# Full contraction depth for every matmul, and a part of the output scaling moved to ScalarE

## The chip, the core and the metric

The kernel runs on one core of a Trainium2 chip. The metric is the device time of one execution in microseconds. The kernel before takes 212.89 us, the median of three runs (211.91 to 213.91); one execution that was recorded by the profiler spans 211.2 us from the first to the last instruction.

## The reference

The input `A_u` is a sequence of 2048 positions with 512 channels. Two layers work on it, and a gate mixes them:

```python
x = A_u                                            # (1, 2048, 512), bf16
g = sigmoid((x * gate_w).sum(-1, keepdims=True))
a = conv(x)                                        # long convolution, below
b = x + scatter(two routed tokens)                 # below
return g * a + (1 - g) * b

# conv: a kernel of 2048 taps per channel, from 128 complex modes
K = einsum("dn,dnl,dn->dl", C, exp(dt * A * l), dt * B).real
y = irfft(rfft(pad(x)) * rfft(pad(K)))[:L] + x * Dskip

# routing: the two positions with the largest x @ w_r pass a gated MLP
y = (silu(x_sel @ w_gate) * (x_sel @ w_up)) @ w_down * sigmoid(r_sel)
b = x + scatter_add(y at the two positions)
```

The kernel does the Fourier transforms as matmuls with constant cosine and sine tables, in two blocks of 1024 positions and two halves of 256 channels. The taps are the product of two small tables of exponentials: one over coarse lags, one over fine lags.

## The kernel before

The kernel has a small scheduler of its own. Each step is recorded with the buffers that it reads and writes and with a cost; a list scheduler then decides the order on each engine, and for some steps also the engine (`EV`, an eviction from PSUM, and `SCL`, a scaling, may go to ScalarE or to VectorE). [...] So a change of a cost or of a step can change the order of the whole program. The helpers `TT`, `STT`, `CP` are VectorE operations, `AC` is a ScalarE activation; because a helper records the operation, the profile gives them all the helper's line (387 for `TT`, 394 for `STT`, 398 for `AC`, 402 for `EV`, 406 for `SCL`).

The order of the parts in the program, cut to what the steps below touch:

```python
exps1(0); exps2(0)       # all exponentials, ScalarE
# ... a part of them is parked in HBM ("park") and read back for the second half
routing()                # transposes of x, gate, the top two, the MLP
tab1(0, (1, 1))          # sine and cosine times exponentials: coarse table, half 0
forward()                # Fourier transform of x
tab2(0, (1, 1))          # fine table, half 0
tab1(1, (1, 1))
xupd()                   # x + routed rows, scaled by 1 - g
kgen(0)                  # product of the tables, then selection
# ... DMA of the spectrum matrix KP and of the parked table
tab2(1, (1, 1))
kspec(0)                 # spectrum of the taps, half 0
kgen(1)
products(0, 0); products(0, 1)   # spectrum products, VectorE
# ... DMA of the inverse matrix G
kspec(1)
inverse(0)               # inverse transform, gate and add
products(1, 0); products(1, 1)
inverse(1)
```

In the product of the tables and the selection, a group of lags is brought together onto 32 partitions; the identity matrix, every fourth column of it, is the stationary operand. The first of the four groups also takes `Dskip` in, by a matmul of one row:

```python
def kgen(h):
    # ... 64 x 2 matmuls of 84 columns in 11 groups, each evicted to KA[h]
    for bk in range(3):
        pb = misc()
        def sel(hh, bk=bk, pb=pb):
            njg = 2 if bk < 2 else 1
            for g in range(4):
                for c4 in range(4):
                    lw = CB(0, 128, c4, (4, 32))
                    last = hh.matmul(pb(32 * g, 32, c4, (256, njg), (4, 64)), lw, KA[h](...),
                                     start=True, stop=(bk + g > 0), tile_position=(0, 32 * g))      # line 767
                    if bk + g == 0:
                        last = hh.matmul(pb(0, 32, c4, (4, 64)), CB(0, 1, 0, (1, 32)), DSK(0, 1, h * HC + c4, (4, 64)),
                                         start=False, stop=True, tile_position=(0, 0))              # line 770
            if bk == 2:
                for c4 in range(4):
                    last = hh.matmul(pb(0, 32, 256 + c4, (4, 64)), CB(0, 128, c4, (4, 32)), KA[h](...),
                                     start=True, stop=True, tile_position=(0, 0))                   # line 773
        # ... bk 0 and 1 evicted whole; bk 2 in two pieces, of 128 and of 32 partitions
```

The spectrum of the taps uses blocks of 128 rows, and for the last block (the single lag 2048 steps on) 32 rows. `KUSE` has five uses for `i == 0`, all of 128 rows, and two for `i == 1`, of 128 and of 32 rows:

```python
KUSE = [(0, 0), (0, 1), (0, 2), (0, 3), (0, 4), (1, 4), (1, 5)]
def kspec(h):
    for qd in range(2):
        for i in range(2):
            # ... for each of two parts, four rows of the spectrum:
            for n, tau in enumerate(taus):
                for k, u in enumerate(uses):
                    jg = KUSE[u][1]
                    np_ = 128 if jg < 5 else 32
                    last = hh.matmul(pb(0, 128, n * 256, (1, 256)), KP(0, np_, ...), KC[h](0, np_, jg * 256, (1, 256)), ...)  # line 795
```

The update with the routed rows alternates a matmul of 128 rows and one of two rows, and ScalarE scales the sum:

```python
def xupd():
    for tb in range(16):
        # pb: one of two PSUM buffers, c0: one of its halves
        h.matmul(pb(0, 128, c0, (1, D)), IDN(0, (1, 128)), U(0, 128, tb * D, (1, D)), start=True, stop=False)          # line 871
        h.matmul(pb(0, 128, c0, (1, D)), OHR(0, 2, tb * 128, (1, 128)), ZB(0, 2, D, (1, D)), start=False, stop=True)   # line 872
        AC(U(...), pb(...), ACTF.Copy, ..., scale=SG(0, 128, 48 + tb, (1, 1)))
```

The inverse transform is 16 matmuls for each group of two tiles of positions (line 845). For the first half of the channels ScalarE scales with the gate into `YA`, and VectorE adds four tiles at once. For the second half VectorE does both in one operation per tile:

```python
if h == 0:
    for e in range(2):
        AC(YA(...), pb(...), ACTF.Copy, ..., scale=SG(0, 128, 32 + tb, (1, 1)))
    if t2 == 1:
        u = U(0, 128, (blk * 8 + par) * D, (2 * D, 4), (1, HC))
        TT(u, u, YA(0, 128, par * 1024, (HC, 4), (1, HC)), ADD, ...)
    continue
for e in range(2):
    STT(u, pb(0, 128, e * 256, (1, 256)), SG(0, 128, 32 + tb, (1, 1)), u, MUL, ADD, ...)
```

Of the kernel before, what the change touches and what calls it, by code (L numbers as in the profile page):

```python
# [326 lines left out]
def bass_gated_mix__ssm_conv_s4__moe_arch_mod__prompt_kernel(nc, A_u, A_A_re, A_A_im, A_B_re, A_B_im, A_C_re, A_C_im, A_log_dt, A_Dskip,  # L327
# [4 lines left out]
    sgn = np.diag(np.where(np.arange(128) % 2 == 0, 1.0, -1.0))  # L332
    cb = np.concatenate([eye, sgn, -sgn], 1)
    cb_c = const(cb, "c_bf")
# [17 lines left out]
    with ExitStack() as es:  # L352
# [59 lines left out]
        def small(name, nbytes, dt):  # L412
            b = B(name, o_[0], nbytes, dt)
            o_[0] += (nbytes + 31) // 32 * 32
            return b
        CB = small("cb", 768, BF); CF = small("cf", 640, F32); AL = small("al", 2048, F32); B16 = small("b16", 2048, F32)
        WW = small("ww", 2048, BF); SG = small("sg", 256, F32); SGB = small("sgb", 128, BF); RTS = small("rts", 1088, F32)
# [66 lines left out]
        DQ([(LDT(0, 128, 0, (1, D)), dr(A_log_dt, 0, (0, 128), (1, D)))], [], [LDT], 131072, eng=ACT)  # L484
        DQ([(CB(0, 128, 0, (1, 384)), cb_c[:, :])], [], [CB], 98304, eng=ACT)
        P.op(ACT, ld_w, [], [WL], cost=1.0, n=2, nbytes=20000, dma=True, prio=2.5e5)
# [8 lines left out]
        for ft in range(2):  # L495
            DQ([(NG[ft](0, 128, 0, (128, 8), (1, 128)), ngsrc(ft))], [], [NG[ft]], 262144)
        DQ([(WG(0, 128, 0, (NF, 4), (1, NF)), dr(B_w_gate, 0, (NF, 128), (128 * NF, 4), (1, NF)))], [], [WG], 1835008)
        DQ([(DSK(0, 1, 0, (1, D)), dr(A_Dskip, 0, (D, 1), (1, D)))], [], [DSK], 1024)

# [116 lines left out]
        def routing():  # L616
            for q in range(8):
                bb = misc(True)
                def tr(h, q=q, bb=bb):
                    last = None  # L620
                    for t_ in range(2):
                        for db in range(4):
                            last = h.transpose(bb(0, 128, db * 256 + t_ * 128, (1, 128)), U(0, 128, (2 * q + t_) * D + db * 128, (1, 128)), IDN(0, (1, 128)))  # L623
                    return last
                P.op(PE, tr, [(U, 2 * q), (U, 2 * q + 1), CB], [bb.buf], cost=0.7)
                EV(XT(0, 128, q * 256, (L, 4), (1, 256)), bb(0, 128, 0, (256, 4), (1, 256)), [bb.buf], [(XT, q)])
            b = misc()
            def lg(h):
# [7 lines left out]
                return last  # L636
            P.op(PE, lg, [XT, WL], [b.buf], cost=64 * 0.03)
            CP(SGB(0, 128, 0, (1, 16)), b(0, 128, 0, (2, 16)), [b.buf], [(SGB, "s")])
# [33 lines left out]
            def gat(h):  # L672
# [4 lines left out]
                return last  # L677
            P.op(PE, gat, [U, OHT], [gb.buf], cost=64 * 0.03)
            CP(XS(0, 128, 0, (1, 8)), gb(0, 128, 0, (1, 8)), [gb.buf], [XS])
            for hf in range(2):  # L680
                bb = misc(True)
                def tro(h, bb=bb, hf=hf):
                    last = None
                    for t_ in range(8):
                        last = h.transpose(bb(0, 2, t_ * 128, (1, 128)), OHT(0, 128, (hf * 8 + t_) * 2, (1, 2)), IDN(0, (1, 128)))
                    return last
                P.op(PE, tro, [OHT, CB], [bb.buf], cost=0.7)
                EV(OHR(0, 2, hf * 1024, (1, 1024)), bb(0, 2, 0, (1, 1024)), [bb.buf], [(OHR, hf)])
# [3 lines left out]
            for i, (W, k) in enumerate(((wg, [WG]), (wu, WU))):  # L692
                bb = misc()
                def ffn1(h, W=W, bb=bb):
                    last = None
                    for fb in range(14):
                        for db in range(4):
                            last = h.matmul(bb(0, 128, fb * 2, (1, 2)), W(db, fb), XS(0, 128, db * 2, (1, 2)), start=(db == 0), stop=(db == 3))
                    return last
                P.op(PE, ffn1, [*k, XS], [bb.buf], cost=56 * 0.035)  # L700
                CP(hb(i), bb(0, 128, 0, (1, 28)), [bb.buf], [(HB, i)])
# [4 lines left out]
            def dn(h):  # L706
# [3 lines left out]
                return last  # L710
            P.op(PE, dn, [(HB, 3), WD], [yb.buf], cost=14 * 0.24)
            CP(ZB(0, 2, 0, (1, D)), yb(0, 2, 0, (1, D)), [yb.buf], [(ZB, 0)])
# [3 lines left out]
        def forward():  # L716
            np_ = [0]
            for blk in range(NBLK):
                for ft in range(4):
# [4 lines left out]
                    for pm in range(2):  # L724
                        pb = fwp[np_[0] % 2]
                        np_[0] += 1
                        for part in range(2):
                            def fw(h, blk=blk, ft=ft, pm=pm, pb=pb, ng=ng, part=part):
# [6 lines left out]
                                if blk:  # L735
                                    last = h.matmul(o, CB(0, 128, 128 * (2 if part == 0 else 1), (1, 128)),
                                                    X(0, 128, (1 - part) * 2048 + (pm * 4 + ft) * 256, (8192, 2), (1, 256)), start=False, stop=True)
                                return last
                            rd = [F, CB, ng] + [(U, blk * 8 + t) for t in range(8)]
                            if blk:  # L740
                                rd += [xk(hh, 0, 1 - part, pm, ft) for hh in range(2)]
                            P.op(PE, fw, rd, [(pb.buf, part)], cost=(8 + blk) * 0.22)
                        EV(X(0, 128, blk * 4096 + (pm * 4 + ft) * 256, (2048, 2), (8192, 2), (1, 256)), pb(0, 128, 0, (512, 2), (256, 2), (1, 256)),
                           [pb.buf], [xk(hh, blk, part, pm, ft) for hh in range(2) for part in range(2)])

        def kgen(h):
            for b0 in range(0, 64, 6):
                ng = min(6, 64 - b0)
                pb = kgp[(b0 // 6) % 2]
                def mm(hh, b0=b0, ng=ng, pb=pb):  # L750
# [5 lines left out]
                    return last  # L756
                P.op(PE, mm, [*TP[h], *TQ[h]], [pb.buf], cost=ng * 2 * 0.05)
                EV(KA[h](0, 128, b0 * 84, (1, ng * 84)), pb(0, 128, 0, (1, ng * 84)), [pb.buf], [(KA[h], b0)])
            for bk in range(3):
                pb = misc()  # L760
                def sel(hh, bk=bk, pb=pb):
                    last = None
# [4 lines that stand above are left out]
                            last = hh.matmul(pb(32 * g, 32, c4, (256, njg), (4, 64)), lw, KA[h](0, 128, c4 + 4 * (8 * bk + g), (16, njg), (84, 64)),  # L767
                                             start=True, stop=(bk + g > 0), tile_position=(0, 32 * g))
                            if bk + g == 0:
                                last = hh.matmul(pb(0, 32, c4, (4, 64)), CB(0, 1, 0, (1, 32)), DSK(0, 1, h * HC + c4, (4, 64)), start=False, stop=True, tile_position=(0, 0))  # L770
                    if bk == 2:
                        for c4 in range(4):
                            last = hh.matmul(pb(0, 32, 256 + c4, (4, 64)), CB(0, 128, c4, (4, 32)), KA[h](0, 128, c4 + 80, (84, 64)),
                                             start=True, stop=True, tile_position=(0, 0))
                    return last
                P.op(PE, sel, [KA[h], CB, DSK], [pb.buf], cost=16 * 0.09)
                if bk < 2:
                    EV(KC[h](0, 128, bk * 512, (1, 512)), pb(0, 128, 0, (1, 512)), [pb.buf], [(KC[h], bk)])
                else:
                    EV(KC[h](0, 128, 1024, (1, 256)), pb(0, 128, 0, (1, 256)), [pb.buf], [(KC[h], 2)])  # L780
                    EV(KC[h](0, 32, 1280, (1, 256)), pb(0, 32, 256, (1, 256)), [pb.buf], [(KC[h], 3)])
        def kspec(h):
            for qd in range(2):
                for i in range(2):
                    uses = [u for u, (bi, jg) in enumerate(KUSE) if bi == i]
                    pb = fwp[i]
                    for part in range(2):
                        taus = [part * 8 + pm * 4 + 2 * qd + e for pm in range(2) for e in range(2)]
                        def ks(hh, taus=taus, uses=uses, pb=pb):
                            last = None  # L790
                            for n, tau in enumerate(taus):
                                for k, u in enumerate(uses):
                                    jg = KUSE[u][1]
                                    np_ = 128 if jg < 5 else 32
                                    last = hh.matmul(pb(0, 128, n * 256, (1, 256)), KP(0, np_, u * 2048 + tau * 128, (1, 128)), KC[h](0, np_, jg * 256, (1, 256)), start=(k == 0), stop=(k == len(uses) - 1))  # L795
                            return last
                        P.op(PE, ks, [KP, KC[h]], [pb.buf], cost=4 * len(uses) * 0.115)
                        o = KK[h](0, 128, i * 4096 + part * 2048 + 2 * qd * 256, (1024, 2), (1, 512))
# [35 lines left out]
        def inverse(h):  # L834
            for blk in (1, 0):
                for par in range(2):
                    for t2 in range(2):
                        pb = ivb[ni[0] % 4]
                        ni[0] += 1
                        def iv(hh, blk=blk, par=par, t2=t2, pb=pb):  # L840
# [6 lines left out]
                            return last  # L847
                        P.op(PE, iv, [G] + [xk(h, blk, part, par, ft) for part in range(2) for ft in range(4)], [pb.buf], cost=16 * 0.115)
                        if h == 0:
                            for e in range(2):  # L850
                                tb = blk * 8 + (2 * t2 + e) * 2 + par
                                AC(YA(0, 128, (2 * t2 + e) * 256 + par * 1024, (1, HC)), pb(0, 128, e * 256, (1, HC)), ACTF.Copy, [pb.buf, (SG, "g")], [(YA, (par, t2, e))], scale=SG(0, 128, 32 + tb, (1, 1)))
                            if t2 == 1:
                                tbs = [blk * 8 + s_ * 2 + par for s_ in range(4)]
                                u = U(0, 128, (blk * 8 + par) * D, (2 * D, 4), (1, HC))
                                TT(u, u, YA(0, 128, par * 1024, (HC, 4), (1, HC)), ADD, [(YA, (par, a_, e)) for a_ in range(2) for e in range(2)] + [(U, ("x", tb)) for tb in tbs], [(U, ("o", tb, h)) for tb in tbs])
# [9 lines left out]
        def xupd():  # L866
            for tb in range(16):
                pb = fwp[(tb // 2) % 2]
                c0 = (tb % 2) * 512
                def xu(h, tb=tb, pb=pb, c0=c0):  # L870
                    h.matmul(pb(0, 128, c0, (1, D)), IDN(0, (1, 128)), U(0, 128, tb * D, (1, D)), start=True, stop=False)  # L871
                    return h.matmul(pb(0, 128, c0, (1, D)), OHR(0, 2, tb * 128, (1, 128)), ZB(0, 2, D, (1, D)), start=False, stop=True)  # L872
                P.op(PE, xu, [(U, tb), CB, OHR, (ZB, 1)], [(pb.buf, tb % 2)], cost=0.5)
# [81 lines left out]
```

## Time and profile before

| | before |
|---|---|
| time, median of 3 | 212.89 us (211.91 to 213.91) |
| span of the profiled execution | 211.2 us |
| TensorE (PE) busy | 180.4 us, 1490 matmuls |
| TensorE weight loads (PEld) busy | 109.8 us |
| VectorE (DVE) busy | 173.8 us |
| ScalarE (ACT) busy | 138.1 us |
| mean granted TensorE clock | 0.911 |
| spectrum matmuls of 32 rows | 32, 278 ns mean |
| selection: 128 rows / 1 row | 96 + 8 of line 773 / 8 |
| update: 128 rows / 2 rows | 16 / 16 |

Three engines are busy for most of the span, in a program of several stages, so the shares say little. A matmul's duration in the records is from its start to the modelled end of its passage through the array; matmuls overlap, and what a stream of them costs is the distance between starts. "Idle before" is the time that an engine stood still ahead of an instruction, with the engine or DMA that ended it behind the arrow. TensorE's granted clock is 1.00 or 0.50 at any moment; a figure between is the mean of a stretch.

By stage: the exponentials on ScalarE fill the first 34 us. From 36 to 99 us VectorE (60.2 of 62.9 us) and ScalarE (58.9) build the tables while TensorE does the forward transform. Then come selection, update and spectrum of the first half, the tables of the second half, products and inverse transforms.

### The profile page before, as it was taken

How to read it: one execution, taken by the hardware profiler on the slowest of the kernel's cores; microseconds unless marked ns; L12 is line 12 of the kernel's file. 1: busy time of each engine (PE TensorE's matmuls, PEld its weight loads, DVE VectorE, ACT ScalarE, POOL GpSimd, SP SyncE). 2: the span in 40 equal slices, each digit the busy share in tenths (PEclk: the TensorE clock that was granted, in tenths of full speed). 3: DMA queues.
4: the chain of work that ended last, by engine and by line, in shares of the span. 5: the costliest groups of instructions: out<-in, count | busy, mean ns of one | idle time of the engine just before them, and what ended most of it. 6: DMA issues, size and time to landing. Idle time of an engine off the chain costs nothing.

```text
span 211.2 us, 3613 instructions
## 1 busy us (share of the span) xinstructions
PE 180.4 (85%) x1490; PEld 109.8 (52%) x1490; DVE 173.8 (82%) x292; ACT 138.1 (65%) x221; POOL 0.2 (0%) x4
## 2 busy tenths in 40 slices
PE   0294999999999999997997999849889999936992
PEld 0273446743444444463341366529556777825882
DVE  0889465999999999975259969999997969998952
ACT  3899999999889996999279745526534455430000
POOL 0000000000000000000000000000000000000000
PEclk9996699979999999999797589975969999996999
DMA  5999996290202201001990000000370000213033
GB/s 96 357 286 350 373 388 205 55 339 7 50 4 49 50 7 42 3 0 25 432 429 14 0 3 0 0 0 3 90 310 0 0 3 0 73 30 99 0 99 99
DMA packets 22097, 23.08 MB, mean 109 GB/s; under 512 B 13121, under 2 KB 19394, under 8 KB 21442
## 3 DMA queue, kind: packets, MB, share of 16 engines
q1 hardware_dynamic: 20738, 22.63, 32.4%
q10 hardware_dynamic: 1344, 0.23, 0.9%
q8 instruction: 11, 0.18, 0.4%
q14 instruction: 4, 0.03, 0.0%
HBM read 18.93 MB, written 3.15 MB: 105 GB/s over the span
## 4 chain that ended last, share of the span: by engine, by line
DVE 40%; PE 32%; ACT 22%; DMA 3%; SPq 1%; issue 1%; DVEq 0%
DVE AR L387 33%; ACT AR L398 15%; PE ps L845 9%; PE ps L795 8%; ACT AR L402 5%; PE ps L767 4%; PE ps L754 3%; DVE AR L391 3%; DMA AR<-in_A_u_dram 3%; PE ps L623 2%; PE ps L734 2%; PE ps L872 1%; PE ps L871 1%; DVE AR L402 1%; DVE AR L406 1%; SPq L483 1%
## 5 line engine op out<-in xcount | busy, mean ns | idle before, releaser
L387 DVE TENSOR_TENSOR AR<-AR 128x1024 bf16<-128x1024 bf16 (+6 forms) x182 | 134.6, 798 | 19.2 <-DMA AR<-in_A_A_re_dram 5.2
L402 ACT ACTIVATE AR<-ps 128x1024 bf16<-128x1024 f32 (+7 forms) x59 | 45.5, 787 | 34.0 <-PE ps L795 19.9
L734 PE MATMUL ps<-AR 128*128 128x512 bf16 x256 | 63.3, 400 | 0.0
L398 ACT ACTIVATE AR<-AR 128x512 bf16<-128x512 f32 (+3 forms) x84 | 59.3, 770 | 5.2 <-DVE AR L391 3.7
L734 PEld LDWEIGHTS ps<-AR 128*128 128x128 bf16 x256 | 25.6, 102 | 31.6 <-issue 5.9
L795 PE MATMUL ps<-AR 128*128 128x256 bf16 x224 | 33.8, 288 | 1.8 <-ACT AR L402 1.8
L845 PE MATMUL ps<-AR 128*128 128x256 bf16 x256 | 30.2, 282 | 4.9 <-DVE AR L387 4.9
L845 PEld LDWEIGHTS ps<-AR 128*128 128x128 bf16 x256 | 25.5, 101 | 9.1 <-DVE AR L387 5.2
L795 PEld LDWEIGHTS ps<-AR 128*128 128x128 bf16 x224 | 22.2, 101 | 13.6 <-ACT AR L402 2.6
L398 ACT ACTIVATE AR<-ps,AR 128x512 bf16<-128x512 f32 (+1 forms) x32 | 17.1, 582 | 7.4 <-PE ps L845 7.0
L406 ACT ACTIVATE AR<-AR 128x256 int32<-128x256 f32 (+1 forms) x44 | 19.1, 492 | 0.2
L754 PE MATMUL ps<-AR 128*128 128x84 bf16 x256 | 13.8, 221 | 4.9 <-DVE AR L387 2.9
L754 PEld LDWEIGHTS ps<-AR 128*128 128x128 bf16 x256 | 12.6, 110 | 7.7 <-ACT AR L402 3.7
L623 PE MATMUL ps<-AR 128*128 128x128 bf16 x64 | 6.4, 278 | 9.9 <-DMA AR<-in_A_u_dram 9.4
L391 DVE TENSOR_SCALAR AR<-AR 128x1024 int32<-128x1024 int32 (+4 forms) x24 | 13.2, 550 | 0.3
L623 PEld LDWEIGHTS ps<-AR 128*128 128x128 bf16 x64 | 5.4, 127 | 10.8 <-DMA AR<-in_A_u_dram 9.4
L394 DVE SCALAR_TENSOR_TENSOR AR<-ps,AR 128x256 bf16<-128x256 f32 x16 | 7.0, 478 | 4.6 <-PE ps L845 4.6
L406 DVE TENSOR_SCALAR AR<-AR 128x256 int32<-128x256 f32 (+1 forms) x28 | 7.0, 292 | 2.8 <-ACT AR L398 2.7
L767 PE MATMUL ps<-AR 128*32 128x128 bf16 (+1 forms) x96 | 8.4, 381 | 0.7 <-ACT AR L402 0.7
L402 DVE CAST AR<-ps 128x1024 bf16<-128x1024 f32 (+1 forms) x6 | 6.7, 1124 | 2.1 <-PE ps L734 2.1
L871 PE MATMUL ps<-AR 128*128 128x512 bf16 x16 | 7.3, 455 | 1.3 <-ACT AR L398 1.3
L872 PE MATMUL ps<-AR 2*128 2x512 bf16 x16 | 7.4, 465 | 0.0
(35 smaller groups left out, 54.4 us busy)
## 6 DMA issues: line engine op xcount, KB each, us to landing
AR<-c_ksp SPq DMA_DIRECT2D x1, 3584.0 KB, 13.8
AR<-in_A_u_dram SPq DMA_DIRECT2D x2, 1024.0 KB, 7.0
AR<-c_fwd SPq DMA_DIRECT2D x1, 2048.0 KB, 8.1
AR<-c_fwdn SPq DMA_DIRECT2D x8, 256.0 KB, 3.9
AR<-c_inv SPq DMA_DIRECT2D x1, 2048.0 KB, 7.8
out_dram<-AR SPq DMA_DIRECT2D x16, 128.0 KB, 2.2
AR<-in_B_w_gate_dram SPq DMA_DIRECT2D x1, 1792.0 KB, 11.0
AR<-in_B_w_up_dram SPq DMA_DIRECT2D x2, 896.0 KB, 11.4
```

What stands on the lines that cost most here:

```text
L387: return P.op(DVE, lambda h: h.tensor_tensor(out=o, in0=a, in1=b, op=op), rd, wr, cost=tt_cost(o, a, b), **k)
L391: return P.op(DVE, lambda h: h.tensor_scalar(out=o, in0=a, scalar1=s1, scalar2=None, op0=op0), rd, wr, cost=c, **k)
L398: return P.op(ACT, lambda h: h.activation(out=o, in_=a, func=func, scale=scale, bias=bias), rd, wr, cost=0.185 + nel(o) * 0.833e-3 + (0.09 ...
L402: return P.op((ACT, DVE), (lambda h: h.activation(out=o, in_=a, func=ACTF.Copy), lambda h: h.tensor_copy(o, a)), rd, wr, cost=(0.185 + n * ...
L406: return P.op((ACT, DVE), (lambda h: h.activation(out=o, in_=a, func=ACTF.Copy, scale=c), lambda h: h.tensor_scalar(out=o, in0=a, scalar1= ...
L623: last = h.transpose(bb(0, 128, db * 256 + t_ * 128, (1, 128)), U(0, 128, (2 * q + t_) * D + db * 128, (1, 128)), IDN(0, (1, 128)))
L734: last = h.matmul(o, w, U(0, 128, (blk * 8 + st * 2 + par) * D, (1, D)), start=(par + st == 0), stop=(par * 4 + st == 7 and blk == 0))
L754: last = hh.matmul(pb(0, 128, (g - b0) * 84, (1, 84)), TP[h][1 - part](0, 128, g * 128, (1, 128)), TQ[h][1 - part](0, 128, g * 84, (1, 84) ...
L767: last = hh.matmul(pb(32 * g, 32, c4, (256, njg), (4, 64)), lw, KA[h](0, 128, c4 + 4 * (8 * bk + g), (16, njg), (84, 64)), start=True, sto ...
L795: last = hh.matmul(pb(0, 128, n * 256, (1, 256)), KP(0, np_, u * 2048 + tau * 128, (1, 128)), KC[h](0, np_, jg * 256, (1, 256)), start=(k ...
L845: last = hh.matmul(pb(0, 128, e * 256, (1, 256)), G(0, 128, ((par * 2 + part) * 4 + ft) * 512 + (2 * t2 + e) * 128, (1, 128)), X(0, 128, h ...
L872: return h.matmul(pb(0, 128, c0, (1, D)), OHR(0, 2, tb * 128, (1, 128)), ZB(0, 2, D, (1, D)), start=False, stop=True)
```

## The change

Every matmul is given 128 rows. The one-row skip operand, the two-row one-hot operands and the 32-row spectrum operands are held in buffers of 128 partitions whose other rows are zero: `DSK`, `OHR` and `ZB` are cleared by GpSimd at the start, and the last selection group is written to all 128 partitions by a stationary operand that has zero columns beyond the 32 (the identity table gets 384 zero columns for it). The sums are the same. [...] Besides, the scaling of one of the two blocks of the second half goes to ScalarE, as in the first half, and a dozen costs for the scheduler are new.

```diff
-    cb = np.concatenate([eye, sgn, -sgn], 1)
+    cb = np.concatenate([eye, np.zeros((128, 384), np.float32), sgn, -sgn], 1)
...
+        for buf, n in ((DSK, D), (OHR, L), (ZB, 2 * D)):
+            P.op(POOL, lambda h, buf=buf, n=n: h.memset(buf(0, 128, 0, (1, n)), 0.0), [], [buf], cost=0.2 + n * 0.5e-3)
...
-                P.op(PE, tr, [(U, 2 * q), (U, 2 * q + 1), CB], [bb.buf], cost=0.7)
+                P.op(PE, tr, [(U, 2 * q), (U, 2 * q + 1), CB], [bb.buf], cost=0.9)
... (costs of the logits, gather, MLP, forward, table, spectrum and inverse matmuls: 1 to 26% lower)
-                P.op(PE, tro, [OHT, CB], [bb.buf], cost=0.7)
+                P.op(PE, tro, [OHT, CB], [bb.buf], cost=0.5)
...
-  last = hh.matmul(pb(0, 32, c4, (4, 64)), CB(0, 1, 0, (1, 32)), DSK(0, 1, h * HC + c4, (4, 64)), start=False, stop=True, tile_position=(0, 0))
+  last = hh.matmul(pb(0, 32, c4, (4, 64)), CB(0, 128, 0, (1, 32)), DSK(0, 128, h * HC + c4, (4, 64)), start=False, stop=True, tile_position=(0, 0))
...
-  last = hh.matmul(pb(0, 32, 256 + c4, (4, 64)), CB(0, 128, c4, (4, 32)), KA[h](0, 128, c4 + 80, (84, 64)), start=True, stop=True, tile_position=(0, 0))
+  last = hh.matmul(pb(0, 128, 256 + c4, (4, 64)), CB(0, 128, c4, (4, 128)), KA[h](0, 128, c4 + 80, (84, 64)), start=True, stop=True)
...
-                if bk < 2:
-                    EV(KC[h](0, 128, bk * 512, (1, 512)), ...)
-                else:
-                    EV(KC[h](0, 128, 1024, (1, 256)), ...)
-                    EV(KC[h](0, 32, 1280, (1, 256)), ...)
+                EV(KC[h](0, 128, bk * 512, (1, 512)), ...)
...
-                                    np_ = 128 if jg < 5 else 32
-  last = hh.matmul(pb(...), KP(0, np_, u * 2048 + tau * 128, (1, 128)), KC[h](0, np_, jg * 256, (1, 256)), ...)
+  last = hh.matmul(pb(...), KP(0, 128, u * 2048 + tau * 128, (1, 128)), KC[h](0, 128, jg * 256, (1, 256)), ...)
...
-                        if h == 0:
+                        if h == 0 or blk == 1:
...
-  return h.matmul(pb(0, 128, c0, (1, D)), OHR(0, 2, tb * 128, (1, 128)), ZB(0, 2, D, (1, D)), start=False, stop=True)
+  return h.matmul(pb(0, 128, c0, (1, D)), OHR(0, 128, tb * 128, (1, 128)), ZB(0, 128, D, (1, D)), start=False, stop=True)
```

Ahead of the change ScalarE evicts two of the eight groups of transposes of x among its exponentials, and after it three; the order of the table matmuls, the update and the last forward blocks differs too.

## The prediction

> **What bounds the kernel now.** I read first the chain that ended last, by engine: VectorE carries 40% of it, although TensorE is busy longer. Then the timeline of VectorE alone, where a bracket gives the idle time before a piece and who ended it. These lines are the whole pieces from 98.9 us on that begin with idle time, up to the last stretch:
>
> ```profile
> 103.90 1.29 DVE L387 TENSOR_TENSOR AR<-AR 128x1024 bf16<-128x1024 bf16 x2 [4.95 <-DMA AR<-park]
> 108.20 3.10 DVE L387 TENSOR_TENSOR AR<-AR 128x1024 bf16<-128x1024 bf16 x5 [3.01 <-PE ps L773]
> ...
> 124.79 1.83 DVE L387 TENSOR_TENSOR AR<-AR 128x2048 bf16<-128x2048 bf16 x2 [1.82 <-ACT AR L402]
> ...
> 162.09 9.43 DVE L387 TENSOR_TENSOR AR<-AR 128x2048 bf16<-128x2048 bf16 x10 [1.56 <-ACT AR L402]
> 173.28 21.19 DVE L387 TENSOR_TENSOR AR<-AR 128x1024 bf16<-128x1024 bf16 x26 [1.76 <-ACT AR L398]
> ```
>
> VectorE works from 36.3 to 194.5 us with hardly another gap. So TensorE matters where it ends one of these gaps, and in the last stretch: from 191.66 us TensorE runs 128 matmuls in 15.76 us and everything waits for them. The third view is the chain in order of time, around the second gap (selection, line 767; its K=1 skip matmul, line 770) and the third (first group of the spectrum, line 795):
>
> ```profile
> 103.25 0.33 PE ps L767
> 103.58 0.15 PE ps L770
> ...
> 105.20 2.54 PE ps L767 x42
> 107.74 0.44 PE ps L773 x4
> ...
> 119.59 4.12 PE ps L795 x20
> 123.71 0.02 issue
> 123.73 1.03 ACT AR L402
> ```
>
> A selection matmul beside a K=1 one costs 0.33 and its partner 0.15 us; 42 of them without partners take 0.06 us each. The same is seen in two stretches of equal clock, counted by windows (the count is that of matmuls): full-depth matmuls of 256 columns, and the alternation of K=128 with K=32:
>
> ```profile
> 161.04:163.02 1.98, 1.98 (x20) 1.00 0.00 0
> 163.02:164.71 1.69, 1.69 (x11) 1.00 0.00 0
> ```
>
> The single starts in the trace are 0.109 us apart in the first stretch and 0.211 to 0.216 us in the second. The routing update (lines 871 and 872, K=128 and K=2) steps by 0.32 us per 512-column matmul at full clock, where the plain forward stream steps by about 0.216 (8 in 1.89 us less the pipeline's tail). In each case an alternation adds about 0.10 us per matmul.
>
> [...] the 0.10 us above is paid exactly where the number of rows changes[...]. [...] Here 2x128 loads take 93 ns and 128x128 ones 99 to 102, so zero rows cost nothing by themselves. [...] The windows' granted clock here is 0.50 or 1.00; TensorE ran 116 to 124 us fully "busy" at 0.50 and 0.59, with the K=2 alternation in it. [...]
>
> **The change, part by part.**
>
> 1. Spectrum. 32 of 224 matmuls go from 32 to 128 rows; each stands beside a 128-row one, 8 of 28 per group. Per group 8 x (0.211-0.109) = 0.8 us, 8 groups: 6.5 us of TensorE time.
> 2. Selection. Four pairs took 4 x 0.48 = 1.93 us. As 8 equal matmuls on one column tile they take 0.06 each (the row of 42) to 0.12 each (L773, four on one tile): 0.5 to 1.0. Saved 0.9 to 1.4, say 1.3 us, twice. The last four, now 128 columns wide, I leave equal; one eviction instead of two (0.60 against 0.64).
> 3. Routing update: 32 matmuls x 0.10 = 3.4 us of TensorE time, but ScalarE's eviction (0.58 net each) sets much of that pace.
> 4. Scaling of one of the two blocks of the second half: 8 VectorE pieces of 0.48 become 8 ScalarE pieces of 0.47 and two adds of 0.6. In the last stretch TensorE steps 0.109 us x 128 whatever VectorE does: worth 0.
> 5. Zero fills on GpSimd: it is otherwise empty, and they come before any reader. Identity table 192 instead of 96 KB: at 345 GB/s about 0.3 us for the first input behind it.
> 6. The scheduler's costs change, so the order changes. Evictions of the transposes on ScalarE go from 2 to 3 before the exponentials end. ScalarE is the chain there, so +0.9 us, and about +0.3 us for waiting for that transpose (the second one now comes early). VectorE now runs two one-hot evictions (0.6 each) ahead of the negated sine at 36.31 us. The table stretch starts about 1.6 us later; VectorE has three 0.2 us scalings fewer, so about +1.0 remains at 83 us.
>
> **From there to the end.** At 83 us ScalarE takes over. Up to the last kernel-table eviction the new order removes from it two cosines and one sine (2.9), five scalings (1.5), one forward eviction (0.9), adds three update evictions (1.8), and makes it wait some 2.3 us for a forward block that is now ahead of the tables. Adding its pieces from 82.4 us gives the last table matmul at 98.3, against 99.03 now.
>
> After it: an update pair, one forward block (1.95 us at full clock, 3.45 at half, as at 99.5 to 103 now), then selection 4.9-1.3 = 3.6, gives 104.4 to 105.9; the parked table's DMA (lands 4.8 us after issue) and one 1.13 us eviction that VectorE gets put its restart at 104.5 in any case. Now it is 108.20. I take 105.2: **-3.0**.
>
> From the selection's end VectorE has 14.8 us of work, plus one 0.6 us multiply that now comes before it: 15.4. The first spectrum eviction was ready 16.6 us after the selection's end. In the new order ScalarE does the last update evictions by 12.3, TensorE needs 2.2 us warm or 4.1 cold for 20 matmuls, and the eviction 1.0: 14 to 16. The 1.82 us gap shrinks to about nothing: 16.6-15.4 = **-1.2**.
>
> For the gap at 162.09 VectorE waits for the second spectrum group. TensorE's path to it loses 1.3 (selection) and 0.8 (first 8 of K=32), 2.1 against a gap of 1.56: **-1.6**. For the gap at 173.28 (scaled output of the first half) TensorE's path loses two more groups of 8, 1.6 us, and has 0.5 left over from the gap before (2.1-1.6): enough for the whole 1.76 if all goes well. I take **-1.5**.
>
> In the last stretch TensorE then stands idle longer than the present 4.9 us, and it begins at half clock, now for 3.3 us (16 matmuls at 0.21 instead of 0.11, 1.6 us lost). [...] **+0.6**.
>
> Sum: -3.0-1.2-1.6-1.5+0.6 = -6.7, from 212.89: **206.2 us**.
>
> **Rivals.** (a) The gaps are filled by other waits. For it: VectorE is at 96% from 36 to 99 us and nothing there is removed, every gap has a second arrival close behind, and the DMA of the parked table caps the first. Then 1 or 2 us remain: 211. Against: all four arrivals come from TensorE's stream in stages that the change shortens.
> (b) The order costs more at the front than the gaps give: ScalarE +1.2, VectorE +1.6 before 40 us, and ScalarE saturated to 99. If none of it is recovered by the table evictions, the second gap gains 1 instead of 3: 208 to 210.
> (c) The clock. The clock falls to half seven times before the end. If full rows count as busier, the update and first spectrum stay at full clock from 108 to 124 us, and TensorE's path there is 4 us shorter. But VectorE's 15.4 us is already the longer path, so little more comes; only a warm selection stage and a warm table stretch would help, 203 to 204. Against a general gain: the half-clock windows at 140 and 191 us follow idle time, which remains.
> (d) The moved scaling is the main thing: it would show as an earlier end of the last stretch. TensorE's unbroken 15.74 us there speaks against it.
>
> **Range and chances.** The gaps add to 8.1 us from 108 on; all gained and the front free is 203.5; half gained with a late front is 209.5. Eight in ten: 203.3 to 209.8. The 2% line is 208.6; I put 0.80 on faster, 0.17 within, 0.03 slower, the last because nothing added is long.
>
> **What would show it.** Spectrum matmuls all 0.109 us apart, and no 1- or 2-row form; selection in about 3.6 us; VectorE's four gaps of 3.0, 1.8, 1.6, 1.8 us at most 0.5 each; last stretch of 15.5 to 17.5 us of TensorE as before. I am wrong if zero-padded matmuls keep the 0.2 us step [...], if VectorE's restart after the selection is later than 107 us, or if new gaps of over 1 us stand in VectorE between 40 and 90 us.

## The result, and the profile after

| | before | after |
|---|---|---|
| time, median of 4 | 212.44 us (211.91 to 213.91) | 205.55 us (205.34 to 207.2) |
| ratio, with 95% interval | | 0.9682 [0.9609, 0.9754] |
| span of the profiled execution | 211.2 us | 203.5 us |
| last stretch (128 matmuls) begins | 191.66 us | 183.08 us |
| mean granted TensorE clock | 0.911 | 0.921 |

The change is worth 6.9 us of the medians. The predicted 206.2 us is 0.65 us too high, and the range holds the result.

VectorE's timeline after the change, columns as before: start, length, what, and in brackets the idle time ahead of the piece and who ended it.

```profile
104.64 4.30 DVE L387 TENSOR_TENSOR AR<-AR 128x1024 bf16<-128x1024 bf16 x7 [0.58 <-PE ps L775]
...
114.88 73.67 DVE L387 TENSOR_TENSOR AR<-AR 128x1024 bf16<-128x1024 bf16 x96
190.18 0.69 DVE L387 TENSOR_TENSOR AR<-AR 128x1024 bf16<-128x1024 bf16 x1 [1.63 <-ACT AR L398]
```

The wait of 3.01 us for the selection is 0.58 us, and VectorE restarts at 104.64 us instead of 108.20. The three gaps after it (1.82, 1.56, 1.76 us) have no successors: one unbroken piece of 73.67 us reaches to 188.5 us, into the last stretch. This accounts for the difference of the two profiled executions. The restart is 3.56 us earlier, the three gaps give 5.14, and the rest of VectorE's time between the restart and the last stretch is 0.12 longer (78.44 us, against 83.46 less 5.14). Together 8.58 us, which is 191.66 less 183.08. The last stretch gives 0.92 back; 7.66 us remain, the difference of the spans.

The chain in order of time, around the first selection (line 769; 772 is the former one-row matmul, 775 the last group), the spectrum (791) and the last stretch (841), columns start, length, what:

```profile
98.92 1.73 PE ps L736 x8
...
100.87 0.33 PE ps L769
101.20 0.06 PE ps L772
101.26 0.24 PE ps L769
101.50 0.06 PE ps L772
101.56 2.45 PE ps L769 x43
104.01 0.61 PE ps L775 x4
...
158.85 3.06 PE ps L791 x28
...
183.08 16.68 PE ps L841 x128
```

The same parts of the chain before (734 is the forward transform, 795 the spectrum, 845 the inverse transform):

```profile
99.60 3.43 PE ps L734 x8
...
166.74 3.78 PE ps L795 x28
...
191.66 15.76 PE ps L845 x128
```

The former one-row matmul takes 0.06 us instead of 0.15, and the matmul behind it 0.24 instead of 0.33. A selection takes 3.75 us instead of 4.9. A group of 28 spectrum matmuls takes 3.06 us, 0.109 each; before it took 3.78. Only the last four of the selection are dearer, 0.61 us against 0.44. The last stretch is 16.68 us, against 15.76.

Not all of the earlier restart belongs to the change. The 3.56 us divide into 0.59 for the earlier end of the table matmuls, 0.09 for an update pair, 1.18 for the selection, and 1.70 for the eight forward matmuls between them, which ran at half clock before (3.43 us) and at full clock after (1.73). The kernel with the moved scaling alone (below), which has the order of the kernel before up to there, ran this block at full clock, and its VectorE waited 1.34 us for the selection instead of 3.01. First its chain, then its VectorE:

```profile
99.80 1.83 PE ps L734 x8
```

```profile
106.80 3.10 DVE L387 TENSOR_TENSOR AR<-AR 128x1024 bf16<-128x1024 bf16 x5 [1.34 <-PE ps L773]
```

Against that execution the restart is 2.16 us earlier, and the spans differ by 5.8 us (209.4 against 203.5).

The chain by engine, from the page:

```profile
PE 63%; DVE 22%; ACT 7%; DMA 4%; issue 1%; SPq 1%; DVEq 0%
```

Before, VectorE had 40% of it. It has not become idle (171.3 us busy, 173.8 before). The share follows the order of the program and not the length of the waits: in the new order with the short rows back, where the waits are back too, TensorE has 69%, and in the old order with full rows VectorE has 55%.

### The profile page after: what moved, and what is told of

It is laid out like the page before. It is cut to its first block, busy times and chain, and to the rows that moved or that the text cites. A ratio compares the mean times of both kernels' runs of the same rounds, so it can differ in the third digit from the quotient of the medians.

```text
span 203.5 us, 3609 instructions
## 1 busy us (share of the span) xinstructions
PE 163.9 (81%) x1479; PEld 108.6 (53%) x1490; DVE 171.3 (84%) x281; ACT 141.1 (69%) x232; POOL 3.4 (2%) x7
## 4 chain that ended last, share of the span: by engine, by line
PE 63%; DVE 22%; ACT 7%; DMA 4%; issue 1%; SPq 1%; DVEq 0%
PE ps L736 28%; DVE AR L387 20%; PE ps L841 12%; PE ps L791 6%; PE ps L756 5%; ACT AR L402 4%; DMA AR<-in_A_u_dram 4%; PE ps L769 3%; ACT AR L398 3%; PE ps L738 2%; PE ps L711 2%; PE ps L625 1%; PE ps L700 1%; SPq L483 1%; PE ps L637 1%
## 5 line engine op out<-in xcount | busy, mean ns | idle before, releaser
L387 DVE TENSOR_TENSOR AR<-AR 128x1024 bf16<-128x1024 bf16 (+7 forms) x184 | 135.7, 797 | 12.5 <-DMA AR<-in_A_A_re_dram 6.8
L398 ACT ACTIVATE AR<-AR 128x512 bf16<-128x512 f32 (+4 forms) x84 | 59.5, 769 | 5.4 <-DVE AR L391 2.1
L402 ACT ACTIVATE AR<-ps 128x1024 bf16<-128x1024 f32 (+4 forms) x56 | 44.0, 811 | 25.5 <-PE ps L791 12.8
L736 PE MATMUL ps<-AR 128*128 128x512 bf16 x248 | 59.0, 388 | 0.8 <-issue 0.5
L841 PE MATMUL ps<-AR 128*128 128x256 bf16 x256 | 31.1, 287 | 5.9 <-DVE AR L387 5.9
L398 ACT ACTIVATE AR<-ps,AR 128x256 bf16<-128x256 f32 (+1 forms) x40 | 20.4, 565 | 18.8 <-PE ps L841 18.8
L841 PEld LDWEIGHTS ps<-AR 128*128 128x128 bf16 x256 | 26.3, 103 | 10.2 <-DVE AR L387 6.2
L791 PE MATMUL ps<-AR 128*128 128x256 bf16 x224 | 26.1, 274 | 1.7 <-ACT AR L402 1.7
L406 ACT ACTIVATE AR<-AR 128x256 int32<-128x256 f32 (+1 forms) x50 | 21.1, 484 | 0.1
L867 PE MATMUL ps<-AR 128*128 128x512 bf16 x13 | 6.4, 492 | 3.6 <-ACT AR L398 3.6
L868 PE MATMUL ps<-AR 128*128 128x512 bf16 x16 | 7.6, 474 | 0.2
L406 DVE TENSOR_SCALAR AR<-AR 128x256 int32<-128x256 f32 (+1 forms) x22 | 5.6, 296 | 1.9 <-ACT AR L398 1.8
L769 PE MATMUL ps<-AR 128*32 128x128 bf16 (+1 forms) x96 | 6.4, 383 | 0.5 <-ACT AR L402 0.5
L402 DVE COPY AR<-ps 128x1024 bf16<-128x1024 bf16 (+1 forms) x7 | 4.7, 686 | 1.7 <-PE ps L625 1.4
```

What stands on the lines that cost most here:

```text
L387: return P.op(DVE, lambda h: h.tensor_tensor(out=o, in0=a, in1=b, op=op), rd, wr, cost=tt_cost(o, a, b), **k)
L398: return P.op(ACT, lambda h: h.activation(out=o, in_=a, func=func, scale=scale, bias=bias), rd, wr, cost=0.185 + nel(o) * 0.833e-3 + (0.09 ...
L402: return P.op((ACT, DVE), (lambda h: h.activation(out=o, in_=a, func=ACTF.Copy), lambda h: h.tensor_copy(o, a)), rd, wr, cost=(0.185 + n * ...
L406: return P.op((ACT, DVE), (lambda h: h.activation(out=o, in_=a, func=ACTF.Copy, scale=c), lambda h: h.tensor_scalar(out=o, in0=a, scalar1= ...
L736: last = h.matmul(o, w, U(0, 128, (blk * 8 + st * 2 + par) * D, (1, D)), start=(par + st == 0), stop=(par * 4 + st == 7 and blk == 0))
L791: last = hh.matmul(pb(0, 128, n * 256, (1, 256)), KP(0, 128, u * 2048 + tau * 128, (1, 128)), KC[h](0, 128, jg * 256, (1, 256)), start=(k ...
```

## Experiments

All times are medians, with the ratio to the kernel before, run beside it on the same chip, and its 95% interval. The kernel before had 211.85 to 212.41 us there. The changed kernel was not run again beside them; its 205.55 us stand against 212.44 for the kernel before, so a difference from it of 0.6 us or less shows nothing.

### The short rows back, in the new order

The order of the instructions is that of the changed kernel; only the row counts are the old ones. The 128 columns of the last selection group, the larger table, the zero fills and the moved scaling stay.

```diff
-CB(0, 128, 0, (1, 32)), DSK(0, 128, h * HC + c4, (4, 64))
+CB(0, 1, 0, (1, 32)), DSK(0, 1, h * HC + c4, (4, 64))
-OHR(0, 128, tb * 128, (1, 128)), ZB(0, 128, D, (1, D))
+OHR(0, 2, tb * 128, (1, 128)), ZB(0, 2, D, (1, D))
-KP(0, 128, ...), KC[h](0, 128, jg * 256, (1, 256))
+KP(0, 128 if jg < 5 else 32, ...), KC[h](0, 128 if jg < 5 else 32, jg * 256, (1, 256))
```

> The changed kernel, its order untouched, with the short rows back in all three places: one-row skip matmul, two-row one-hot matmul, 32-row spectrum matmul. If the depth is what brings the gain, by way of VectorE's waits, it loses most of it: the selection takes about 0.7 us longer, the spectrum group 0.8, VectorE waits again at the second half's first spectrum product and at the gated add; 209.5 to 211.5 us. If the new order of the program brings it, the time stays below 207.

Measured 214.29 us, ratio 1.0111 [1.0056, 1.0167]: more than expected, and slower than the kernel before. VectorE's timeline of this kernel has all the gaps again:

```profile
107.76 4.30 DVE L387 TENSOR_TENSOR AR<-AR 128x1024 bf16<-128x1024 bf16 x7 [2.11 <-PE ps L775]
...
124.48 35.49 DVE L387 TENSOR_TENSOR AR<-AR 128x2048 bf16<-128x2048 bf16 x48 [1.34 <-ACT AR L402]
161.69 9.44 DVE L387 TENSOR_TENSOR AR<-AR 128x2048 bf16<-128x2048 bf16 x10 [1.71 <-ACT AR L402]
172.88 6.51 DVE L387 TENSOR_TENSOR AR<-AR 128x1024 bf16<-128x1024 bf16 x8 [1.76 <-ACT AR L398]
180.27 17.44 DVE L387 TENSOR_TENSOR AR<-AR 128x1024 bf16<-128x1024 bf16 x22 [0.88 <-ACT AR L398]
```

The restart is 3.1 us later than in the changed kernel and the four gaps add 5.7. Of the 3.1 us, 1.05 are there already at the first table matmul (88.66 us, against 87.61), where the two kernels are still the same. So the contraction depth is worth about 8.7 us in this order by the medians (214.29 less 205.55), and what is left of the change without it (order, costs, larger table, fills, moved scaling) loses 2.4 us.

### The full rows in the old order

The kernel before, with its own costs and order and all operands of 128 rows, the larger identity table and the zero fills included.

> The kernel before, its order and costs untouched, with all matmuls at 128 rows and nothing else. Depth theory: VectorE's gaps of 3.0, 1.8, 1.6 and 1.8 us shrink to about 1.5, 0.5, 0.3 and 0.3; 206.5 to 209. Order theory: 211 or more.

Measured 207.31 us, ratio 0.9765 [0.9696, 0.9834], as expected. VectorE's timeline, around the selection's end and after it:

```profile
106.30 4.38 DVE L387 TENSOR_TENSOR AR<-AR 128x1024 bf16<-128x1024 bf16 x7 [4.96 <-DMA AR<-park]
...
116.60 71.75 DVE L387 TENSOR_TENSOR AR<-AR 128x1024 bf16<-128x1024 bf16 x93
```

The depth alone closes the three later gaps, and the wait for the selection as well: the seven multiplications run without a break, where before a wait of 3.01 us stood between the second and the third. What it doesn't give in this order is an earlier start of the seven: that is put down to the read-back of the parked table, which lands 5.1 us after the start of the last table matmul here (101.21 us) as it does before (98.83, landing at 103.90). The last table matmul is 2.4 us late, and so is the end of the exponentials (36.10 us, against 33.73). This is where depth and order depend on each other: the rest of the change without the depth loses 2.4, the depth with its table and fills alone gains 4.5, and both together gain 6.9.

### The moved scaling, taken out and done alone

```diff
-if h == 0 or blk == 1:
+if h == 0:
```

> The changed kernel with the output scaling of the second half back on VectorE. TensorE's 128 matmuls set the last stretch, so I expect no difference: 205.5 within 0.7. The rival, that the moved scaling shortens the last stretch, expects 206.5 or more.

Measured 206.19 us (206.03 to 206.71), ratio 0.9735 [0.968, 0.9789]. It is 0.6 us above the changed kernel, with overlapping intervals. The reverse edit in the kernel before:

> The kernel before with the moved scaling and nothing else. No difference expected: 212.4 within 0.7. The rival expects 211.4 or less.

Measured 211.82 us, ratio 1.0007 [0.9983, 1.003] over 20 executions: no difference. The moved scaling is not what made the change fast.

### 32 rows in the spectrum only

```diff
+np_ = 128 if jg < 5 else 32
-KP(0, 128, ...), KC[h](0, 128, jg * 256, (1, 256))
+KP(0, np_, ...), KC[h](0, np_, jg * 256, (1, 256))
```

> The changed kernel with 32 rows again in 32 of the 224 spectrum matmuls only. Switch theory: each group of 8 takes 0.8 us longer, VectorE waits again at the second half's first products and at the gated add: 2 us more, 207.5 (206.5 to 208.5). Rival, TensorE has slack enough there by now: no more than 0.5 us.

Measured 209.24 us, ratio 0.9872 [0.9824, 0.9919]: 3.7 us above the changed kernel, where 2 were expected. VectorE's timeline:

```profile
115.56 40.31 DVE L387 TENSOR_TENSOR AR<-AR 128x1024 bf16<-128x1024 bf16 x56
156.13 9.44 DVE L387 TENSOR_TENSOR AR<-AR 128x2048 bf16<-128x2048 bf16 x10 [0.26 <-ACT AR L402]
167.32 6.51 DVE L387 TENSOR_TENSOR AR<-AR 128x1024 bf16<-128x1024 bf16 x8 [1.76 <-ACT AR L398]
174.71 17.44 DVE L387 TENSOR_TENSOR AR<-AR 128x1024 bf16<-128x1024 bf16 x22 [0.88 <-ACT AR L398]
```

The gap at the first half's scaled output is back at its old 1.76 us, with one of 0.88 behind it. Together with the 0.26 that makes 2.9 us; the remaining 0.7 is in the restart (105.33 us, against 104.64), ahead of any spectrum matmul, and so not the edit's.

### The 32-row matmuls side by side

The same matmuls as in the last kernel, but in the order 128, 128, 32, 32 instead of 128, 32, 128, 32: half as many changes of row count, equally many short matmuls.

```diff
-for n, tau in enumerate(taus):
-    for k, u in enumerate(uses):
+seq = [...] if len(uses) > 2 else [(n + m, k) for n in (0, 1) for k in (0, 1) for m in (0, 2)]
+for n, k in seq:
```

> As the run before, but with the matmuls of a group of 8 in pairs: two of 128 rows, two of 32, two of 128, two of 32; so there are half as many changes of the row count and as many short matmuls. If the cost sits on the change, a group of 8 goes from 1.7 us to about 1.3; if it sits on each short matmul and its neighbour, it stays at 1.7; if on each short matmul alone, too.

Measured 207.19 us, ratio 0.9795 [0.9739, 0.9852]. TensorE's timeline of the two kernels, first the alternating one (791 is the spectrum, 841 the inverse transform behind it), then the paired one (792, 842):

```profile
160.61 3.95 PE L791 MATMUL ps<-AR 128*128 128x256 bf16 x28
164.49 1.92 PE L841 MATMUL ps<-AR 128*128 128x256 bf16 x16
```

```profile
159.91 3.53 PE L792 MATMUL ps<-AR 128*128 128x256 bf16 x28
163.37 1.92 PE L842 MATMUL ps<-AR 128*128 128x256 bf16 x16
```

From start to start a group of 28 takes 3.88 us alternating, 3.46 in pairs, and 3.06 at full depth. The single steps of the paired kernel at full clock say why (medians): 0.204 us from 128 to 32 rows, 0.12 from 32 to 32, 0.20 from 32 to 128, 0.12 from 128 to 128 in such a group. Four changes in a group of 8 instead of eight make about 1.3 us, as expected for a cost on the change. The cost sits on the change, and a short matmul beside a short one costs no more than a long one beside a long one (0.12 us each). The two gaps are half of what they were (0.92 and 0.46 us, against 1.76 and 0.88).

### Two rows in the update only

```diff
-OHR(0, 128, tb * 128, (1, 128)), ZB(0, 128, D, (1, D))
+OHR(0, 2, tb * 128, (1, 128)), ZB(0, 2, D, (1, D))
```

> The changed kernel with two-row one-hot operands again in the 16 updates only. TensorE steps 0.32 instead of 0.216 us in them. Switch theory: selection ends 0.5 us later for the updates ahead of it, and the rest lengthens VectorE's way to the first spectrum product by up to 1: 206 to 207.2. If the clock is the point, one more stretch of half clock appears at 110 to 124 us than in the changed kernel.

Measured 208.79 us, ratio 0.984 [0.9766, 0.9914]: 3.2 us above the changed kernel, where at most 1.7 were expected. In VectorE's timeline the gap ahead of the first spectrum product is back:

```profile
116.60 5.13 DVE L387 TENSOR_TENSOR AR<-AR 128x1024 bf16<-128x1024 bf16 x8
123.81 44.85 DVE L387 TENSOR_TENSOR AR<-AR 128x2048 bf16<-128x2048 bf16 x58 [2.08 <-ACT AR L402]
```

TensorE's timeline says where that comes from; first the changed kernel (867 has always 128 rows, 868 is the one-hot matmul), then this one:

```profile
115.18 0.63 PE L867 MATMUL ps<-AR 128*128 128x512 bf16 x1
115.61 0.63 PE L868 MATMUL ps<-AR 128*128 128x512 bf16 x1
116.04 3.50 PE L791 MATMUL ps<-AR 128*128 128x256 bf16 x28
```

```profile
117.49 0.61 PE L867 MATMUL ps<-AR 128*128 128x512 bf16 x1
118.03 0.60 PE L868 MATMUL ps<-AR 2*128 2x512 bf16 x1
118.57 5.03 PE L791 MATMUL ps<-AR 128*128 128x256 bf16 x28
```

Both update stretches are at half clock, where a step is 0.43 us at full depth and 0.54 with the alternation. TensorE runs the last pairs without a pause, so it sets the update's end here, and not ScalarE's eviction as I had assumed. The half clock also lasts longer. In three kernels with the two-row update (the one before, this one, and the one with short rows everywhere) it lasts 10.2 us between 111 and 124 us. In five with full rows it is shorter: 6.8 us in the changed kernel (109.8 to 116.6), about 3.4 in the two spectrum edits and in the one with unread matmuls (below), by the steps of their update matmuls, and 0 in the old order. The first 28 spectrum matmuls that follow take 5.03 us, where in the changed kernel they take 3.50. The restart after the selection is later too, at 106.36 us instead of 104.64; 1.0 of these 1.7 us is there already at the first table matmul (88.60 us, against 87.61), ahead of every update.

### Unread matmuls ahead of the last stretch

The changed kernel, with 24 matmuls of 512 columns into a free PSUM buffer before the last stretch, where TensorE stands idle for VectorE. Nothing reads them.

```diff
+P.op(PE, warm, [G, ivb[3].buf], [fwp[0].buf], cost=0.1)   # 24 matmuls, ahead of products(1, 0)
```

> The changed kernel with 24 matmuls added that nobody reads, in TensorE's idle time of 5.9 us ahead of the last stretch (about 5.2 us at full clock). They keep the clock up: the last 128 matmuls take 14.0 us instead of 16.7, and the time falls by 2.5 to 203.0 (202.4 to 204). If instead VectorE or ScalarE hold the last stretch, TensorE gets gaps in it and the time falls by less than 1.

Measured 203.79 us (203.46 to 204.2), ratio 0.9618 [0.9571, 0.9664], as expected. Windows of TensorE over the last stretch (length, busy time of PE, PEld, DVE, ACT, POOL with the number of instructions, granted clock, DMA share, GB/s), first the changed kernel, then this one:

```profile
182.00:186.00 4.00, 2.92 (x14) 2.11 (x15) 3.97 (x6) 0.00 (x0) 0.00 (x0) 0.50 0.43 124
186.00:190.00 4.00, 4.00 (x29) 3.16 (x27) 2.52 (x4) 1.53 (x4) 0.00 (x0) 0.71 0.03 8
```

```profile
182.00:186.00 4.00, 3.29 (x25) 2.24 (x24) 4.00 (x7) 0.10 (x1) 0.00 (x0) 1.00 0.26 76
186.00:190.00 4.00, 4.00 (x39) 3.58 (x38) 3.93 (x6) 2.19 (x6) 0.00 (x0) 1.00 0.19 55
```

Without the half clock the 128 matmuls take 14.16 us instead of 16.68, and begin at 183.95 us.

### The late front, and two versions that beat both kernels

In the changed kernel the input's transposes begin at 10.77 us instead of 9.37. Two edits each take away one suspect: the 384 zero columns are filled on GpSimd instead of being loaded (the table is 96 KB again), or the table stays at 192 KB and the fills wait until the input has landed.

```diff
@@ first edit @@
-    cb = np.concatenate([eye, np.zeros((128, 384), np.float32), sgn, -sgn], 1)
+    cb = np.concatenate([sgn, -sgn, eye], 1)     # 384 zero columns behind it by a memset on POOL
@@ second edit @@
-P.op(POOL, lambda h, buf=buf, n=n: h.memset(buf(0, 128, 0, (1, n)), 0.0), [], [buf], cost=0.2 + n * 0.5e-3)
+P.op(POOL, lambda h, buf=buf, n=n: h.memset(buf(0, 128, 0, (1, n)), 0.0), [(U, 15)], [buf], cost=0.2 + n * 0.5e-3)
```

> The changed kernel with the identity table loaded as 96 KB again; its 384 zero columns are cleared by GpSimd (now four fills). In the changed kernel the first parameter transpose lands 1.6 us and the first input block 1.4 us later than before, and the exponentials end 2.5 us later. If the larger load delays them: they land as early as before, and the time falls by 1 to 2 us, to 204.2 (203.5 to 204.9). If the early fills on GpSimd delay them: no change, 205.5.

> The changed kernel with its 192 KB table, and with the three fills of GpSimd put off until the input has landed. If the load delays the start: no change, 205.5 within 0.5. If the fills do: 204.2.

The transposes begin at 9.57 us with the small table and at 9.44 with the late fills: each edit undoes the late landing. But the times are 205.15 us (ratio 0.9682 [0.9643, 0.972]) and 206.09 us (0.9719 [0.9676, 0.9761]), against 205.55: the expected 1 to 2 us don't come. The first table matmul starts at 87.96 and 86.98 us, against 87.61, so most of what the front gains is lost on the way to it. The one profiled execution of each has the clock at half, before 50 us, for 13.7 us with the small table, 10.2 in the changed kernel and 6.8 with the late fills; that goes with the three starts, but it wasn't tried by itself.

Both edits and the 24 unread matmuls together:

> The changed kernel with all three: 96 KB table, late fills, and the 24 matmuls ahead of the last stretch. If the two gains add: 203.8 less 1.5, 202.3 (201.3 to 203.3). If what is won at the start is lost again in the waits for the tables between 84 and 104 us: 203.5 or more.

Measured 202.95 us (202.78 to 203.22), ratio 0.9578 [0.9536, 0.962]. That is below every execution of the kernels with one of the two edits (204.64 and more, on the same chip). Against the 24 matmuls alone, 203.79 us on another chip with an overlapping interval, a gain of the two edits isn't shown. Five more unread matmuls in each of three idle times of TensorE before 40 us:

> The run with all three, and 5 matmuls of 512 columns that nobody reads in each of three early idle times of TensorE (between the last groups of transposes, ahead of the gate's logits and after them). In the chain of the changed kernel TensorE carries the time from 23 to 104 us, and it runs at half clock from 17.6 to 27.8. If the filling keeps the clock up there, the first forward blocks take 1.9 us instead of 3.2 and the time falls by 1 to 2 us, to 201.5. If the logits' matmuls of 2 columns let the clock fall all the same, or the exponentials on ScalarE hold the start anyway, nothing changes: 202.5 to 203.3.

Measured 202.86 us (201.07 to 203.0), ratio 0.9545 [0.9492, 0.9597]. The profiled execution is the lowest of the five: in it the half clock near 20 us is missing (mean granted clock 0.966, against 0.945 to 0.949 in the other four), and the first table matmul starts at 85.71 us. The other four, at 202.68 to 203.0, are no better than without the additions. Whether these added matmuls do anything stays open.

## Why the prediction was right, point by point

- **Spectrum.** The step is 0.109 us at full clock, as predicted. A group saves 0.72 us, for the predicted 0.8, and the edits that bring 32 rows back show that the change of row count costs, not the short matmul: 0.20 us at a change, 0.12 without one. Worth in this order: 2.9 us in the trace of one edit, 3.7 in the medians.
- **Selection.** Predicted 3.6 us, measured 3.75. The part up to the last four went from 4.49 us to 3.14, a saving of 1.35 at the upper end of my 0.9 to 1.4. The last four, which I left equal, became 0.17 us longer as matmuls with 128 columns of weights. The selection's edit alone wasn't tried.
- **Restart after the selection.** Predicted 105.2 us, measured 104.64: -3.56 us for the predicted -3.0. This agreement is in part luck. I had placed the restart between a full-clock and a half-clock forward block, but compared it with an execution of the kernel before that had the half clock just there; 1.70 us of the 3.56 are this clock (1.73 us for eight matmuls, against 3.43). Against an execution with the block at full clock, that of the moved scaling alone, it is 2.16 us.
- **Update.** Here a step was mis-sized: I gave the 32 matmuls 3.4 us of TensorE time, but let ScalarE set the pace. Undone alone it comes out 3.2 us higher in the median, and the half clock lasts longer. Rival (c) was more than I allowed it: the half clock there is 0 to 6.8 us long in five kernels with full rows, against 10.2. I had argued that VectorE's path was the longer one and little more would come; yet the two-row update brings back a gap of 2.08 us on that very path.
- **The three later gaps.** Predicted -1.2, -1.6 and -1.5 us; all of 1.82, 1.56 and 1.76 went. That was the cautious side of each step, 0.84 us in sum.
- **Last stretch.** Predicted +0.6 us for the clock, which was my estimate; measured +0.92. The half clock lasts 6.8 us from 181.5, against 3.4 from 191.6. With the unread matmuls ahead there is no half clock, and the stretch takes 14.16 us: the clock is the cause.
- **Front.** Too optimistic in its terms. The table load was given 0.3 us and the fills none; the transposes of the first input block began 1.4 us late, and 1.0 to 2.0 us late in each of the eight kernels that have both. The end of the exponentials moved by 2.5 us instead of 1.2, the negated sine on VectorE by 3.75 (to 40.06 us) instead of about 1.6. With the input on time (small table) the exponentials end 1.3 us late, which is the predicted 1.2 for the order. None of this showed in the total: the table matmuls end at 98.44 us, where 98.3 was predicted (99.03 before). That the two figures meet so closely is luck too: in the four other profiled kernels that differ from the changed one only later, they end at 99.08 to 99.21. By the prediction's account ScalarE, with its evictions and scalings taken away, makes it good in the table stretch; no run tests that part. Nor are there VectorE gaps above 1 us from 40 to 90 us. So rival (b) names real losses, which don't reach the end in this order. In the old order they do: there the table matmuls were 2.4 us late.
- **Moved scaling.** Nothing that the intervals show, as predicted; rival (d) falls.
- **Rival (a)**, another wait in place of the old one, didn't happen here, but it is what the profile of the full rows in the old order shows: there the parked table's read-back ends VectorE's wait, at 106.30 us. In the changed kernel the read-back is issued at 98.47 us and takes 4.8, so it lands at about 103.3 (an estimate from the two figures), 1.4 us ahead of the restart: this other wait is close behind.

In the profiled executions the sum was 1.0 us short: restart and gaps gave 8.58 us for the predicted 7.3, the last stretch took 0.92 for 0.6, and 7.66 stand against 6.7. In the medians, which take in executions with other granted clocks (0.921 to 0.933 in the four after the change), it is 6.9. So the mechanism, waits of VectorE that TensorE's stream ends, is right, while the sum came this close because errors cancelled: the restart without its clock gave less than predicted, the three later gaps more.

What stays open: why either of the two edits at the start is enough to bring the input on time, and why the end doesn't follow; the selection's share of the time by itself, of which only 1.8 us of the 8.7 are left after the two others (8.7 - 3.7 - 3.2), if the parts simply add; in the traces 0.7 and 1.0 us of those two stand ahead of what the edits touch. In the traces of the new order the first selection takes 5.07 us with short rows and 3.75 without.

## What to carry to other kernels

Padding the contraction rows with zeros cost a matmul nothing here (the median step of the spectrum at full clock is 0.109 us, as it was between full-depth matmuls before) and removed about 0.1 us at each change of row count. It was not free for the program: the larger table together with the early fills made the input 1 to 2 us late. Putting the short matmuls side by side, without padding, removed half of the cost (a group of 28 in 3.46 us, against 3.88 alternating and 3.06 at full depth). Look first for the engine whose idle gaps TensorE ends: TensorE's 0.7 us per group was worth only what VectorE waited, 2.9 us over the eight groups in the trace of the 32-row edit. And look at the clock of a dense last stretch: after 4.9 to 6.2 us of idle time it began at half clock in the two kernels and in five edits of them, and the 128 matmuls took 15.61 to 17.02 us. In two kernels with unread matmuls ahead of it they took 14.16 us, with a granted clock of 1.00 in the windows above. The unread matmuls were worth 1.8 us of the median here.

## What the runs showed of the hardware that I had not expected

- A full-depth matmul following a short one pays as much (0.20 us) as a short one following a full one (0.204); without a change both take 0.12 in that group.
- With the update that alternates 128 and two rows, TensorE is at half clock for 10.2 us there in three of three kernels, though the profile has it busy for 9.6 of them in the kernel before. With full rows it is 0 to 6.8 us in five of five. Each is one profiled execution. What makes the half clock longer isn't shown: no run separates the short rows from the longer stretch that they make.
- In the traces of the two kernels every whole stretch of half clock lasts 3.41, 6.83 or 10.24 us. Its position differs between executions even where the instructions are the same: the eight forward matmuls ahead of the first selection took 3.43 us in the kernel before and 1.83 in the one with the moved scaling alone. This limits what can be read from one execution: the four executions of the kernel with the small table were granted 0.916 to 0.938, and the changed kernel and the one with short rows, which are equal up to the first table matmul, start it at 87.61 and 88.66 us.
- In the eight kernels with the larger table and the early fills together, the input's transposes begin at 10.34 to 11.40 us; in the six that lack one of the two or both, at 9.37 to 10.01. Each figure is one profiled execution.
